# Every second w_in stage of a two-layer kernel by Strassen's scheme: seven half-width products and the additions between them

## The chip, the cores and the metric

The kernel runs on one core of a Trainium2 chip. The metric is the device time of one execution in microseconds. The core has a matrix engine (TensorE, in the profile PE, its weight loads PEld), VectorE (DVE), ScalarE (ACT), GpSimd (POOL) and SyncE (SP), whose queue issues the DMAs. SBUF is the working memory; PSUM, eight banks of 512 floats per partition, takes the matmuls' results.

## The reference, cut to what matters

```
qn = q / (norm(q, axis=1) + 1e-6); kn likewise        # q, k, v: 6016 x 256
a  = softmax(kn.T @ qn / tau)                         # 256 x 256
x  = v @ a                                            # 6016 tokens x 256
h  = x @ w_in;  g = h - tanh(h);  x = g @ w_out       # layer 0, w_in 256 x 2048
h  = x @ w_in2; g = where(h > 0, h, exp(min(h, 0)) - 1); out = g @ w_out2   # layer 1
```

Everything is float32.

## The kernel before

A short attention part makes `a`, and `a` is folded into layer 0's `w_in` (tiles `aw`). The rest is the two layers. The tokens are cut into 12 blocks of 512 columns (the last has 384), and the hidden dimension of 2048 into 8 parts p of 256. One step (layer, b, p) computes the part's h for a block, applies the activation, and adds its share of the output into the block's accumulator `o`; after p = 7 `emit_evac` copies `o` to SBUF (`osb`) and sends it off. Blocks 0 and 1 of layer 0 run interleaved while the weights arrive; from then on the steps run block by block.

Each operand of a matmul is split into a high part, rounded to the matrix engine's 32-bit format, and a low part, the remainder. A product is three matmuls: high by high, high by low, low by high. One step has 2 x 2 tiles of h, so 12 matmuls of 512 columns (`emit_h`, `product`), and 12 for `o` (`emit_out`). Every matmul loads its own 128 x 128 weights. The moving operand is read by `turned`, alternately from the two halves of the block, and the output is numbered accordingly; layer 0's eviction undoes this by a strided write.

The order is written out by hand: the loop over `order` emits h of step s, then `o` of step s - 2 (LAG = 2), then the activation (`emit_act`), and every engine runs its instructions in the order emitted. In layer 0 the activation is tanh on ACT, the subtraction on DVE, the cast to the high part (`ghi`, on DVE from block 3 on) and the low part (`glo`, DVE). In layer 1 it is relu, tanh and exp on ACT, two instructions on DVE (L635, L639), cast and low part on DVE. Both h and `o` have two PSUM buffers of two banks. All weights of both layers stay in SBUF; a `Converter` turns those of layer 1 into parts during layer 0, one unit per step (four DVE instructions, three on ACT, one on POOL).

Of the kernel before, what the change touches and what calls it, by code (L numbers as in the profile page):

```python
# [22 lines left out]
def kernel(  # L23
# [48 lines left out]
    class Converter:  # L72
        def __init__(self, stack, name, n, units, raws, nsq, nlow):
            self.nsq, self.nlow = nsq, nlow
# [39 lines left out]
        def second(self):  # L114

            if self.begun == self.at[1]:
                return []
            s = self.st[self.begun]
            self.begun += 1
            hz = self.tmp.tile([P, self.n], F32, tag="hz", name="hz")  # L120
            cut = self.tmp.tile([P, self.n], U32, tag="cut", name="cut")
# [76 lines left out]
    x_dram = [dram.tile([P, KC, n], F32, name=f"x{b}") for b, (_, n) in enumerate(blocks)]  # L198
    v_of = {}
# [52 lines left out]
    def evac_scalar(ps, m, fs):  # L252
        nc.scalar.activation(
            out=win_hi[0][:, m, fs], in_=ps[:, : 2 * P], func=AF.Copy, scale=rsum[:, m : m + 1]
        )

    def evac_vector(ps, m, fs):
        nc.vector.scalar_tensor_tensor(  # L258
            out=win_lo[0][:, m, fs], in0=ps[:, : 2 * P], scalar=rsum[:, m : m + 1],
            in1=win_hi[0][:, m, fs].bitcast(F32), op0=ALU.mult, op1=ALU.subtract,  # L260
        )
# [223 lines left out]
    with tc.manual_schedule():  # L485
        parts_of = attention()

        wpool2 = ctx.enter_context(tc.tile_pool(name="weights2", bufs=1, side="left"))
        win_hi[1] = wpool2.tile([P, KC, F], F32R, name="win_hi1")
        win_lo[1] = wpool2.tile([P, KC, F], F32R, name="win_lo1")  # L490
        gpool = ctx.enter_context(tc.tile_pool(name="g", bufs=2, side="left"))
        spool = ctx.enter_context(tc.tile_pool(name="s", bufs=2, side="left"))
        opool = ctx.enter_context(tc.tile_pool(name="o", bufs=2, side="left"))
        ps_h = ctx.enter_context(tc.tile_pool(name="ps_h", bufs=2, space=PSUM))
        out_stack = ctx.enter_context(ExitStack())
        ps_o = out_stack.enter_context(tc.tile_pool(name="ps_o", bufs=2, space=PSUM))
# [12 lines left out]
        def fold_attention(p):  # L509

            fs = slice(2 * P * p, 2 * P * (p + 1))
            if p == 1:
                ps = [ps_o.tile([P, 2, 512], F32, tag="o", name=f"aw{p}_{m}")[:, 0] for m in range(KC)]
            else:
                ps = ps_h.tile([P, 2, 512], F32, tag="h", name=f"aw{p}")
                ps = [ps[:, m] for m in range(KC)]
            for m in range(KC):
                if p == 1:
                    fold_half(ps[m], m, next_w, slice(0, 2 * P))
                else:  # L520
                    fold_half(ps[m], m, (win_hi[0], win_lo[0]), fs)
            return ps, fs
# [7 lines left out]
        def emit_h(layer, b, p, last=False):  # L530
            _, n = blocks[b]
            x_hi, x_lo = v_of[layer * NBLK + b]
            h = ps_h.tile([P, 2, 512], F32, tag="h", name=f"h{layer}_{b}_{p}")
# [4 lines left out]
            if layer == 0 and b + p < 2:  # L538

                w_hi, w_lo = [w[0][:, :, 2 * P * p : 2 * P * (p + 1)] for w in (win_hi, win_lo)]  # L540
# [14 lines left out]
            for i in range(2):  # L555
# [5 lines left out]
                            (win_hi[layer][:, c, fs], win_lo[layer][:, c, fs]),  # L561
# [6 lines left out]


        lower = []  # L570

        def emit_act(layer, b, p, h, fold, late=False, full=False):
# [41 lines left out]
            if layer == 0:  # L614
# [9 lines left out]
                if b > 2:  # L624
                    nc.vector.tensor_copy(out=hi, in_=g)  # L625
                else:
                    nc.scalar.activation(out=hi, in_=g, func=AF.Copy)  # L627
            else:

                e = late_pool[0].tile([P, 2, width], F32, tag="e", name="e")[:, :, :n]  # L630
                nc.scalar.activation(out=e, in_=h, func=AF.Relu, scale=-1.0)  # L631
                nc.scalar.activation(out=g, in_=e, func=AF.Tanh, scale=-0.5)  # L632
                nc.scalar.activation(out=e, in_=e, func=AF.Exp, scale=-1.0)  # L633
                between()
# [3 lines left out]
                fill(1)  # L638
                nc.vector.scalar_tensor_tensor(  # L639
                    out=g, in0=h, scalar=0.0, in1=g, op0=ALU.max, op1=ALU.add  # L640
                )
                fill(2)
                nc.vector.tensor_copy(out=hi, in_=g)  # L643
# [4 lines left out]
        def emit_last_act(b, p, h):  # L648
# [6 lines left out]
            for i in range(2):  # L655
                nc.scalar.activation(out=e[:, i], in_=h[i][:, :n], func=AF.Relu, scale=-1.0)
                nc.scalar.activation(out=g[:, i], in_=e[:, i], func=AF.Tanh, scale=-0.5)
                nc.scalar.activation(out=e[:, i], in_=e[:, i], func=AF.Exp, scale=-1.0)
# [4 lines left out]
                    out=g[:, i], in0=h[i][:, :n], scalar=0.0, in1=g[:, i], op0=ALU.max, op1=ALU.add  # L663
# [8 lines left out]
        def emit_last_out(b, p, g):  # L672
# [8 lines left out]
            for w, x, i, c in terms:  # L681
                nc.tensor.matmul(  # L682
                    out=columns(o[c][:, :n]), lhsT=w[1][:, 2 * p + i, c * P : (c + 1) * P],
# [10 lines left out]
        def emit_out(layer, b, p, g):  # L694
            _, n = blocks[b]
            if p == 0:
# [4 lines left out]
                else:  # L701
                    o = ps_o.tile([P, KC, 512], F32, tag="o", name=f"o{layer}_{b}")
# [7 lines left out]
            for w, x in terms:  # L710
                for i in range(2):
                    f = 2 * p + i
                    for c in range(KC):
                        nc.tensor.matmul(  # L714
                            out=columns(o[c][:, :n]),
                            lhsT=w[layer][:, f, c * P : (c + 1) * P],
# [5 lines left out]
        def emit_evac(layer, b, p):  # L722
# [5 lines left out]
            if layer == 0:  # L728

                nc.scalar.activation(  # L730
                    out=s.rearrange("p k (q u) -> p k u q", q=16),
                    in_=o.rearrange("p k (u q) -> p k u q", q=16),
                    func=AF.Copy,
                )
# [30 lines left out]
        for s, (layer, b, p) in list(enumerate(order))[3:]:  # L765
            if conv is not early and conv.done() and not late_pool:
                late_stack.close()
                pool = ctx.enter_context(tc.tile_pool(name="e", bufs=2, side="right"))
                late_pool.append(pool)
            if conv is early and early.done() and s >= starts[-1]:  # L770
                right.close()
                wlate = ctx.enter_context(tc.tile_pool(name="weights_late", bufs=1, side="right"))
                wout_hi[1] = wlate.tile([P, F // P, C], F32R, name="wout_hi1")
                wout_lo[1] = wlate.tile([P, F // P, C], F32R, name="wout_lo1")
                conv = Converter(late_stack, "l", NU // 2, late_units, 3, 1, 3)
# [4 lines left out]
            h = emit_h(layer, b, p, last=(s == len(order) - 1))  # L780
# [6 lines left out]
            if s < len(order) - 1:  # L787
                g = emit_act(layer, b, p, h, fold, full=(s < starts[-1]))
            else:
                g = emit_last_act(b, p, h)  # L790
            pend.append((layer, b, p, g))
            if done:
                emit_evac(*done[:3])

            if s == 3 or (s > 2 * NP and p == 1 and nv < len(phases)):
                load_v(nv)
            if s == 2 * NP - 2 or (s > 2 * NP and p == 4 and nv < len(phases)):
                split_v(nv)
                nv += 1
        emit_out(*pend[0])  # L800
        emit_last_out(*pend[1][1:])

# [34 lines left out]
```

## Time and profile before

| | |
|---|---|
| time, median of 3 runs | 1041.92 us (1041.63 to 1042.25) |
| the profiled execution's own time | 1041.79 us |
| its span in the trace | 1039.7 us |
| PE busy | 1032.8 us, 99% |
| PEld busy | 912.2 us, 88% |
| DVE busy | 842.7 us, 81% |
| ACT busy | 586.9 us, 56% |
| POOL busy | 69.8 us, 7% |

The span is what the trace covers; the time has some 2 us around it. Busy shares are means over all stages.

### The profile page before, as it was taken

How to read it: one execution, taken by the hardware profiler on the slowest of the kernel's cores; microseconds unless marked ns; L12 is line 12 of the kernel's file. 1: busy time of each engine (PE TensorE's matmuls, PEld its weight loads, DVE VectorE, ACT ScalarE, POOL GpSimd, SP SyncE). 2: the span in 40 equal slices, each digit the busy share in tenths (PEclk: the TensorE clock that was granted, in tenths of full speed). 3: DMA queues.
4: the chain of work that ended last, by engine and by line, in shares of the span. 5: the costliest groups of instructions: out<-in, count | busy, mean ns of one | idle time of the engine just before them, and what ended most of it. 6: DMA issues, size and time to landing. Idle time of an engine off the chain costs nothing.

```text
span 1039.7 us, 12840 instructions
## 1 busy us (share of the span) xinstructions
PE 1032.8 (99%) x4954; PEld 912.2 (88%) x4954; DVE 842.7 (81%) x926; ACT 586.9 (56%) x665; POOL 69.8 (7%) x65
## 2 busy tenths in 40 slices
PE   9999999999999999999999999999999999999998
PEld 8888888888888888888898888888888888888898
DVE  7899988888886666666667888888888888888887
ACT  7887776544433223222227666666666666666665
POOL 4522211111110000000000000000000000000000
PEclk9999999999999999999999999999999999999999
DMA  9723032212201101011011001011010010110100
GB/s 348 289 102 102 21 103 80 92 51 91 92 1 41 41 1 41 1 40 36 1 42 36 10 32 41 1 41 41 1 41 19 22 41 1 41 41 1 36 21 16
DMA packets 28381, 54.57 MB, mean 52 GB/s; under 512 B 2464, under 2 KB 7840, under 8 KB 28320
## 3 DMA queue, kind: packets, MB, share of 16 engines
q1 hardware_dynamic: 28032, 53.22, 15.0%
q8 instruction: 39, 0.64, 0.3%
q10 hardware_dynamic: 288, 0.52, 0.1%
q14 instruction: 22, 0.18, 0.1%
HBM read 41.42 MB, written 12.32 MB: 52 GB/s over the span
## 4 chain that ended last, share of the span: by engine, by line
PE 97%; DVE 2%; ACT 1%; issue 0%; DVEq 0%; ACTq 0%
PE h L243 46%; PE o L714 45%; PE S L311 4%; PE aw L243 1%; PE o_last L714 1%; DVE g L598 0%; DVE glo L593 0%; PE warm L323 0%; DVE cut L139 0%; DVE hz L127 0%; DVE cut L146 0%; PE o_last L682 0%; DVE win_lo L258 0%; DVE cut L133 0%; ACT g L597 0%
## 5 line engine op out<-in xcount | busy, mean ns | idle before, releaser
L243 PE MATMUL h<-vhi,win_hi 128*128 128x512 f32 (+1 forms) x754 | 282.5, 375 | 0.7 <-DVE g L598 0.7
L243 PE MATMUL h<-vlo,win_hi 128*128 128x512 f32 (+1 forms) x754 | 282.4, 375 | 0.0
L593 DVE TENSOR_TENSOR glo<-g,ghi 128x1024 fp32r<-128x1024 f32 (+1 forms) x191 | 236.8, 1240 | 22.8 <-ACT ghi L627 4.7
L243 PE MATMUL h<-vhi,win_lo 128*128 128x512 f32 (+1 forms) x754 | 221.0, 375 | 0.0
L615 ACT ACTIVATE g<-h 128x1024 f32<-128x1024 f32 (+1 forms) x82 | 82.3, 1003 | 233.2 <-PE h L243 233.2
L631 ACT ACTIVATE e<-h 128x1024 f32<-128x1024 f32 (+1 forms) x95 | 95.8, 1009 | 162.3 <-PE h L243 162.3
L714 PE MATMUL o<-ghi,wout_hi 128*128 128x512 f32 (+1 forms) x736 | 187.2, 377 | 0.0
L714 PE MATMUL o<-glo,wout_hi 128*128 128x512 f32 (+1 forms) x736 | 187.2, 377 | 0.0
L714 PE MATMUL o<-ghi,wout_lo 128*128 128x512 f32 (+1 forms) x736 | 187.1, 377 | 0.0
L616 DVE TENSOR_TENSOR g<-h,g 128x1024 f32<-128x1024 f32 (+1 forms) x82 | 98.2, 1198 | 93.6 <-ACT g L615 93.5
L243 PEld LDWEIGHTS h<-vhi,win_hi 128*128 128x128 f32 x754 | 142.5, 189 | 19.8 <-ACT wout_hi L166 1.1
L243 PEld LDWEIGHTS h<-vlo,win_hi 128*128 128x128 f32 x754 | 142.5, 189 | 18.6
L243 PEld LDWEIGHTS h<-vhi,win_lo 128*128 128x128 f32 x754 | 141.7, 189 | 18.5
L714 PEld LDWEIGHTS o<-ghi,wout_lo 128*128 128x128 f32 x736 | 138.5, 189 | 18.9
L714 PEld LDWEIGHTS o<-glo,wout_hi 128*128 128x128 f32 x736 | 138.5, 189 | 18.9
L714 PEld LDWEIGHTS o<-ghi,wout_hi 128*128 128x128 f32 x736 | 138.0, 189 | 18.5
L635 DVE SCALAR_TENSOR_TENSOR g<-e,g 128x1024 f32<-128x1024 f32 (+1 forms) x95 | 114.4, 1204 | 36.2 <-ACT e L633 35.6
L639 DVE SCALAR_TENSOR_TENSOR g<-h,g 128x1024 f32<-128x1024 f32 (+1 forms) x95 | 114.5, 1205 | 10.2 <-DVE g L635 0.5
L633 ACT ACTIVATE e<-e 128x1024 f32<-128x1024 f32 (+1 forms) x95 | 99.3, 1046 | 3.0
L632 ACT ACTIVATE g<-e 128x1024 f32<-128x1024 f32 (+1 forms) x95 | 99.3, 1045 | 3.0
L643 DVE CAST ghi<-g 128x1024 fp32r<-128x1024 f32 (+1 forms) x95 | 65.0, 685 | 10.1 <-DVE g L639 0.5
L625 DVE CAST ghi<-g 128x1024 fp32r<-128x1024 f32 (+1 forms) x72 | 48.8, 677 | 5.0
(139 smaller groups left out, 695.1 us busy)
## 6 DMA issues: line engine op xcount, KB each, us to landing
qk<-in_q_dram SPq DMA_DIRECT2D x23, 256.0 KB, 5.2
vraw<-in_vT_dram SPq DMA_DIRECT2D x11, 512.0 KB, 4.6
x<-osb SPq DMA_DIRECT2D x11, 512.0 KB, 3.0
vraw<-x SPq DMA_DIRECT2D x11, 512.0 KB, 4.0
out_dram<-osb SPq DMA_DIRECT2D x11, 512.0 KB, 2.9
qk<-in_k_dram SPq DMA_DIRECT2D x21, 256.0 KB, 5.3
raw0in<-in_moe_w_in_dram SPq DMA_DIRECT2D x8, 512.0 KB, 3.7
raw0out<-in_moe_w_out_dram SPq DMA_DIRECT2D x8, 512.0 KB, 3.7
```

The costliest lines, as they stand in the source:

```text
L243: nc.tensor.matmul(out=out, lhsT=w, rhs=x, start=(i == 0), stop=(i == len(pairs) - 1))
L593: nc.vector.tensor_tensor(out=lo, in0=g, in1=hi.bitcast(F32), op=ALU.subtract)
L615: nc.scalar.activation(out=g, in_=h, func=AF.Tanh)
L616: nc.vector.tensor_tensor(out=g, in0=h, in1=g, op=ALU.subtract)
L625: nc.vector.tensor_copy(out=hi, in_=g)
L631: nc.scalar.activation(out=e, in_=h, func=AF.Relu, scale=-1.0)
L632: nc.scalar.activation(out=g, in_=e, func=AF.Tanh, scale=-0.5)
L633: nc.scalar.activation(out=e, in_=e, func=AF.Exp, scale=-1.0)
L635: nc.vector.scalar_tensor_tensor(out=g, in0=e, scalar=1.0, in1=g, op0=ALU.add, op1=ALU.mult)
L639: nc.vector.scalar_tensor_tensor(out=g, in0=h, scalar=0.0, in1=g, op0=ALU.max, op1=ALU.add)
L643: nc.vector.tensor_copy(out=hi, in_=g)
L714: nc.tensor.matmul(out=columns(o[c][:, :n]), lhsT=w[layer][:, f, c * P : (c + 1) * P], rhs=turned(x[:, i]), start=(f == 0 and w is wout_hi ...
```

## The change

Blocks of 512 columns, from block 3 of layer 0 on and all of layer 1, compute the odd parts p (`PAIRS`) by Strassen's scheme in the Winograd form (`emit_h7`). The 2 x 2 tiles of weights and the 2 x 2 half blocks of tokens are combined to seven products instead of eight half-width ones: 7 x 3 = 21 matmuls of 256 columns into four one-bank tiles q0 to q3. One copy on ACT and four additions on DVE put h together in SBUF (`hs`). The sums of weights (`wsum`) and of tokens (`sum_v`, tiles t, thi, tlo) are made once per part or per block. Even parts stay as they were.

Around this: LAG is 3. From block 2 of layer 0 on, the class `Act` replaces `emit_act`: a plain step is activated in its own step, a Strassen step in the following plain step; the casts are on ACT, and the low part of a Strassen step on POOL. Layer 1's activation is exp and tanh straight from h, and the last DVE instruction takes min and max. PSUM holds q0 to q3 (four banks), one buffer of `o` (`ps_o`) and one of plain h (`ps_b`); plain blocks 0 to 2 and 11 have two h buffers instead of the q tiles. SBUF holds one layer's weights: the converted parts of layer 1 go to DRAM (`Converter.store`) and come back, part by part, during block 11 of layer 0. Conversion units are handled in plain steps only. `turned` now alternates within each half of a block, so layer 0's eviction is two instructions with a shorter stride.

```
+        def emit_h7(layer, b, p):
+            i = layer * NBLK + b
+            xq = [halves(x) for x in v_of[i]]
+            tq = t_of[i]
...
+            q1, q62, q57, q34 = [
+                ps_q[0].tile([P, 512], F32, tag=f"q{k}", name=f"q{k}_{layer}_{b}_{p}") for k in range(4)
+            ]
+            def product7(out, k, weights, moving, first, end):
+                out = out[:, k * W : (k + 1) * W].rearrange("p (l s) -> p l s", s=2)
+                hi, lo = [pair(y[:, moving[1]]) for y in moving[0]]
+                nc.tensor.matmul(out=out, lhsT=weights[0], rhs=hi, start=first, stop=False)
+                nc.tensor.matmul(out=out, lhsT=weights[0], rhs=lo, start=False, stop=False)
+                nc.tensor.matmul(out=out, lhsT=weights[1], rhs=hi, start=False, stop=end)
+            hs = steady[0].tile([P, 8, W], F32, tag="hs", name="hs", bufs=2)
...
+            product7(q1, 0, w(0, 0), (xq, 0), True, True)
+            nc.scalar.activation(out=hs[:, 3], in_=q1[:, :W], func=AF.Copy)
+            product7(q62, 0, ws(1), (tq, 1), True, False)
+            product7(q62, 1, w(1, 0), (xq, 2), False, True)
+            tt(out=hs[:, 0:8:4], in0=quads(q62), in1=two(3), op=ALU.add)
+            product7(q57, 0, ws(0), (tq, 0), True, False)
+            product7(q57, 1, ws(2), (tq, 2), False, True)
+            tt(out=hs[:, 1:3], in0=quads(q57), in1=two(0), op=ALU.add)
+            tt(out=hs[:, 7], in0=q57[:, :W], in1=hs[:, 2], op=ALU.add)
+            product7(q34, 0, ws(3), (xq, 3), True, False)
+            product7(q34, 1, w(1, 1), (tq, 3), False, True)
+            tt(out=hs[:, 5:7], in0=quads(q34), in1=hs[:, 1:3], op=ALU.add)
...
+        class Act:
...
+                    nc.scalar.activation(out=self.e, in_=h, func=AF.Exp)
+                    nc.scalar.activation(out=self.g, in_=h, func=AF.Tanh, scale=0.5)
...
+            def begin(self):
+                if self.layer:
+                    nc.vector.scalar_tensor_tensor(
+                        out=self.g, in0=self.e, scalar=1.0, in1=self.g, op0=ALU.add, op1=ALU.mult
+                    )
+                else:
+                    nc.vector.tensor_tensor(out=self.g, in0=self.h, in1=self.g, op=ALU.subtract)
+            def end(self):
+                if self.layer:
+                    nc.vector.scalar_tensor_tensor(
+                        out=self.g, in0=self.g, scalar=0.0, in1=self.h, op0=ALU.min, op1=ALU.max
+                    )
+            def upper(self):
+                nc.scalar.activation(out=self.hi, in_=self.g, func=AF.Copy)
+            def lower(self):
+                engine = nc.gpsimd if self.apart else nc.vector
+                engine.tensor_tensor(out=self.lo, in0=self.g, in1=self.hi.bitcast(F32), op=ALU.subtract)
...
+            h = emit_h7(layer, b, p) if seven else emit_h(layer, b, p, last=last)
...
+            if seven:
+                before.upper()
+                before.lower()
+                act = Act(layer, b, p, h)
...
+            else:
+                second = conv.second()
...
+                act = Act(layer, b, p, h[2][:, :, : blocks[b][1]])
+                if before and before.apart:
+                    before.begin()
+                    before.end()
+                    before.upper()
+                    before.lower()
...
+                if done:
+                    emit_evac(*done[:3])
+                for fill in second:
+                    fill()
...
+                act.begin()
+                act.end()
...
+                if p == 2:
+                    split_v_scalar(nv)
+                if p == 3:
+                    split_v_rest(nv, nc.vector)
+                apart = strassen(*phases[nv], PAIRS[0])
+                if p == 5 and apart:
+                    sum_v(nv, raw)
+                if p == 7:
+                    if apart:
+                        sum_v_rest(nv, nc.vector)
```

DVE's queue in block 5 of layer 1, before: parts 2 and 3 of that block (`h1_5_3` is h of part 3), with `e` and `g` the tiles of the activation.

```order
L593 TENSOR_TENSOR glo_6155<-g_6153,ghi_6154 128x1024
L635 SCALAR_TENSOR_TENSOR g_6189<-e_6192,g_6189 128x1024
L639 SCALAR_TENSOR_TENSOR g_6189<-h1_5_3_6164,g_6189 128x1024
L643 CAST ghi_6190<-g_6189 128x1024
L593 TENSOR_TENSOR glo_6191<-g_6189,ghi_6190 128x1024
```

The same place of the same queue in the changed kernel: the end of part 1 (Strassen, `hs_7280`), part 2 (plain, `h1_5_2`) and part 3 (Strassen, `hs_7373` from its q tiles).

```order
L712 SCALAR_TENSOR_TENSOR g_7321<-e_7322,g_7321 128x1024
L720 SCALAR_TENSOR_TENSOR g_7321<-g_7321,hs_7280 128x1024
L712 SCALAR_TENSOR_TENSOR g_7352<-e_7353,g_7352 128x1024
L720 SCALAR_TENSOR_TENSOR g_7352<-g_7352,h1_5_2_7327 128x1024
L684 TENSOR_TENSOR hs_7373<-q1_1_5_3_7370,hs_7373 128x2x256
L687 TENSOR_TENSOR hs_7373<-q2_1_5_3_7371,hs_7373 128x512
L688 TENSOR_TENSOR hs_7373<-q2_1_5_3_7371,hs_7373 128x256
L691 TENSOR_TENSOR hs_7373<-q3_1_5_3_7372,hs_7373 128x512
L729 TENSOR_TENSOR glo_7357<-g_7352,ghi_7356 128x1024
L250 TENSOR_TENSOR vlo18_7421<-vraw18_7274,vhi18_7367 128x1024
L712 SCALAR_TENSOR_TENSOR g_7415<-e_7416,g_7415 128x1024
```

The cast and one low part of every two are gone from DVE; four additions have come, and both activations of a pair stand ahead of them.

ACT's queue around the eviction of block 4 (`osb` from `o1_4`), before:

```order
L737 ACTIVATE osb_6122<-o1_4_5842 128x1024
L631 ACTIVATE e_6156<-h1_5_2_6127 128x1024
L632 ACTIVATE g_6153<-e_6156 128x1024
L633 ACTIVATE e_6156<-e_6156 128x1024
L631 ACTIVATE e_6192<-h1_5_3_6164 128x1024
```

And in the changed kernel, where `q0_1_5_3` is the first product of part 3 and `vhi18` the high part of the next block's input:

```order
L706 ACTIVATE g_7321<-hs_7280 128x1024
L705 ACTIVATE e_7353<-h1_5_2_7327 128x1024
L706 ACTIVATE g_7352<-h1_5_2_7327 128x1024
L725 ACTIVATE ghi_7325<-g_7321 128x1024
L893 ACTIVATE osb_7362<-o1_4_7030 128x1024
L243 ACTIVATE vhi18_7367<-vraw18_7274 128x1024
L681 ACTIVATE hs_7373<-q0_1_5_3_7369 128x256
L725 ACTIVATE ghi_7356<-g_7352 128x1024
L705 ACTIVATE e_7416<-hs_7373 128x1024
```

The eviction now stands one step later, behind a cast that needs part 1's activation, and ahead of the copy with which part 3's additions begin.

## Rows read from the trace of the kernel before

**Rows 1.** The page: the span, busy time by engine, a DMA of 512 KB.

```profile
span 1039.7 us, 12840 instructions
...
PE 1032.8 (99%) x4954; PEld 912.2 (88%) x4954; DVE 842.7 (81%) x926; ACT 586.9 (56%) x665; POOL 69.8 (7%) x65
...
vraw<-x SPq DMA_DIRECT2D x11, 512.0 KB, 4.0
...
```

**Rows 2.** Whom TensorE waited for: us in total, times, longest.

```profile
...
PE o_last L682 <- ACT ghi L666: 0.4, 1, 0.4
```

**Rows 3.** Busy us by engine in one stretch of layer 1, then the granted clock.

```profile
...
700.00:800.00 100.00, 100.00 (x465) 87.58 (x464) 86.95 (x80) 64.12 (x62) 0.00 (x0) 1.00 0.06 22
...
```

**Rows 4.** Timeline in layer 1: start us, us, engine, line, operation.

```profile
...
699.57 1.22 DVE L635 SCALAR_TENSOR_TENSOR g<-e,g 128x1024 f32<-128x1024 f32 x1
...
700.75 1.03 PE L714 MATMUL o<-ghi,wout_hi 128*128 128x512 f32 x4
700.89 1.23 DVE L639 SCALAR_TENSOR_TENSOR g<-h,g 128x1024 f32<-128x1024 f32 x1
700.96 1.02 ACT L631 ACTIVATE e<-h 128x1024 f32<-128x1024 f32 x1 [1.97 <-PE h L243]
...
705.93 1.03 PE L714 MATMUL o<-ghi,wout_hi 128*128 128x512 f32 x4
...
```

**Rows 5.** Instruction groups by shape: busy us, mean ns of one, idle before.

```profile
...
L243 PE MATMUL h<-vhi,win_hi 128*128 128x512 f32 x692 | 262.3, 379 | 0.7 <-DVE g L598 0.7
...
L730 ACT ACTIVATE osb<-o 128x1024 f32<-128x1024 f32 x11 | 22.4, 2038 | 11.0 <-PE o L714 11.0
...
L363 POOL TENSOR_TENSOR qk_lo<-qk,qk_hi 128x1024 fp32r<-128x1024 f32 x9 | 21.5, 2384 | 16.1 <-ACT qk_hi L362 14.8 <-DMA qk<-in_k_dram 0.6 <-DVE qk_hi L360 0.6
L243 PE MATMUL h<-vhi,win_hi 128*128 128x384 f32 x62 | 20.2, 326 | 0.0
...
L243 PE MATMUL aw<-next_w,aT_hi 128*128 128x256 f32 x8 | 1.3, 283 | 0.0
...
L466 ACT ACTIVATE aT_hi<-aT_ps 128x256 fp32r<-128x256 f32 x2 | 0.7, 374 | 0.2 <-PE aT_ps L462 0.2
...
L371 DVE TENSOR_TENSOR acc<-sq,acc 128x512 f32<-128x512 f32 x1 | 0.7, 692 | 0.1
...
```

**Rows 6.** Timeline of TensorE in a fold of the attention matrix.

```profile
...
53.94 0.64 PE L243 MATMUL aw<-next_w,aT_hi 128*128 128x256 f32 x4
...
54.66 0.64 PE L243 MATMUL aw<-next_w,aT_hi 128*128 128x256 f32 x4
...
```

**Rows 7.** Timeline of the weight loads near the attention's end.

```profile
...
40.56 0.98 PEld L393 LDWEIGHTS S<-ones,acc 128*128 128x128 f32 x8
...
43.00 0.52 PEld L418 LDWEIGHTS rq_ps<-diag,quot 128*128 128x128 f32 x4
...
```

**Rows 8.** Timeline of DVE and POOL in layer 0.

```profile
...
204.61 1.23 DVE L616 TENSOR_TENSOR g<-h,g 128x1024 f32<-128x1024 f32 x1 [0.62 <-ACT g L615]
...
204.96 0.74 POOL L173 TENSOR_TENSOR win_lo<-cut,win_hi 128x256 fp32r<-128x256 f32 x1 [4.44 <-ACT win_hi L166]
...
205.75 0.28 DVE L133 TENSOR_SCALAR cut<-hz 128x256 uint32<-128x256 uint32 x1
...
```

**Rows 9.** Timeline in layer 0, from DVE to ACT.

```profile
...
149.03 1.23 DVE L616 TENSOR_TENSOR g<-h,g 128x1024 f32<-128x1024 f32 x1 [0.80 <-ACT g L615]
...
150.35 1.06 ACT L627 ACTIVATE ghi<-g 128x1024 fp32r<-128x1024 f32 x1 [0.18 <-DVE g L616]
...
```

**Rows 10.** Timeline of ACT in layer 1, two instructions without a common tile.

```profile
...
609.86 1.06 ACT L633 ACTIVATE e<-e 128x1024 f32<-128x1024 f32 x1
610.83 1.04 ACT L216 ACTIVATE vhi<-vraw 128x1024 fp32r<-128x1024 f32 x1
...
```

**Rows 11.** Timeline of POOL and DVE while the weights are converted.

```profile
...
85.96 1.28 POOL L173 TENSOR_TENSOR win_lo<-cut,win_hi 128x512 fp32r<-128x512 f32 x1 [4.49 <-ACT win_hi L166]
...
86.27 2.06 DVE L593 TENSOR_TENSOR glo<-g,ghi 128x1024 fp32r<-128x1024 f32 x1
...
```

More of the change, by code (lines that the diff above doesn't have):

```diff
@@ L198 @@
     x_dram = [dram.tile([P, KC, n], F32, name=f"x{b}") for b, (_, n) in enumerate(blocks)]
+    in_dram = [dram.tile([P, 2, KC, 2, P], F32, name=f"in{p}") for p in range(NP)]
+    out_dram2 = [dram.tile([P, 2, 2, C], F32, name=f"out{p}") for p in range(NP)]
+    sums_dram = [dram.tile([P, 2, 4, P], F32, name=f"sums{j}") for j in range(len(PAIRS))]
     v_of = {}
@@ L532, in emit_h @@
             x_hi, x_lo = v_of[layer * NBLK + b]
-            h = ps_h.tile([P, 2, 512], F32, tag="h", name=f"h{layer}_{b}_{p}")
+            own = (layer, b) != phases[-1] and strassen(layer, b, 1)
+            h = (ps_b if own else ps_h).tile(
+                [P, 2, 512], F32, tag="o" if own else "h", name=f"h{layer}_{b}_{p}"
+            )
             if last:
@@ L567, in emit_h, with strassen, halves, sums_of @@
             return h
+        steady = []
+        def strassen(layer, b, p):
+            return blocks[b][1] == width and (layer > 0 or b > 2) and p in PAIRS
+        def halves(x):
+            return x.rearrange("p c (h t) -> p (c h) t", h=2)
+        def sums_of(p, first, second, away):
+            j = PAIRS.index(p)
+            t = steady[0].tile([P, 4, P], F32, tag="sum", name="sum")
+            sub = lambda o, a, b, op=ALU.subtract: nc.gpsimd.tensor_tensor(out=t[:, o], in0=a, in1=b, op=op)
+            sub(0, second[:, 0], second[:, 1], ALU.add)
+            sub(2, first[:, 0], second[:, 0])
+            sub(1, t[:, 0], first[:, 0])
+            sub(3, first[:, 1], t[:, 1])
+            dest = steady[0].tile([P, 2, 4, P], F32R, tag="sums_out", name="sums_out") if away else wsum[:, :, j]
+            nc.scalar.activation(out=dest[:, 0], in_=t, func=AF.Copy)
+            nc.gpsimd.tensor_tensor(out=dest[:, 1], in0=t, in1=dest[:, 0].bitcast(F32), op=ALU.subtract)
+            if away:
+                nc.sync.dma_start(out=sums_dram[j], in_=dest.bitcast(F32))
@@ L623, in emit_act @@
                 between()
[L624 to L627, printed above, removed]
+                nc.scalar.activation(out=hi, in_=g, func=AF.Copy)
             else:
                 e = late_pool[0].tile([P, 2, width], F32, tag="e", name="e")[:, :, :n]
[L631 to L634, printed above, removed]
+                nc.scalar.activation(out=e, in_=h, func=AF.Exp)
+                nc.scalar.activation(out=g, in_=h, func=AF.Tanh, scale=0.5)
                 nc.vector.scalar_tensor_tensor(
@@ L728, in emit_evac @@
             if layer == 0:
[L730 to L734, printed above, removed]
+                for c in range(KC):
+                    nc.scalar.activation(
+                        out=s[:, c].rearrange("p (h q u) -> p h u q", h=2, q=16),
+                        in_=o[:, c].rearrange("p (h u q) -> p h u q", h=2, q=16),
+                        func=AF.Copy,
+                    )
                 nc.sync.dma_start(out=x_dram[b], in_=s)
@@ L764 @@
         pend.append((*order[2], emit_act(*order[2], h2, None, full=True)))
[L765 to L769, printed above, removed]
+        for s, (layer, b, p) in list(enumerate(order))[3 : 2 * NP]:
             if conv is early and early.done() and s >= starts[-1]:
                 right.close()
[L772 to L775, printed above, removed]
+                steady.append(ctx.enter_context(tc.tile_pool(name="steady", bufs=1, side="right")))
+                wsum = steady[0].tile([P, 2, len(PAIRS), 4, P], F32R, name="wsum")
+                conv = Converter(late_stack, "l", NU // 2, late_units, 3, 1, 3, 3)
                 conv.load()
@@ L779 @@
                 conv.first()
-            h = emit_h(layer, b, p, last=(s == len(order) - 1))
+            h = emit_h(layer, b, p)
             fold = None
@@ L786 @@
                 emit_out(*done)
[L787 to L791, printed above, removed]
+            pend.append((layer, b, p, emit_act(layer, b, p, h, fold, full=(s < starts[-1]))))
             if done:
                 emit_evac(*done[:3])
-            if s == 3 or (s > 2 * NP and p == 1 and nv < len(phases)):
+            if s == 3:
@@ L800 @@
+        before.upper()
+        before.lower()
+        g = emit_last_act(b, p, h)
         emit_out(*pend[0])
-        emit_last_out(*pend[1][1:])
+        emit_out(*pend[1])
+        emit_last_out(b, p, g)
 def kernel(**inputs):
```

199 lines of the change are left out of this document (163 added, 36 removed).

## The prediction

> **What bounds the kernel now.** I read the page first, then what TensorE waits for, then the stages. TensorE (PE) is busy 1032.8 of the 1039.7 us span [rows 1]; it waits hardly at all, in the last activation for 0.4 us [rows 2]. So the time is the sum of the matmuls, and any other engine counts only if it makes PE wait. In layer 1 VectorE (DVE) is busy 87% and ScalarE (ACT) 64% at full granted clock [rows 3]: DVE is close behind. One plain step runs 5.18 us from one group of `o` matmuls to the next, 24 matmuls of 512 columns, 0.216 us each [rows 4]. The profiled execution took 1041.8 us, 2.1 more than its span, and lies 0.1 below the median of 1041.9; the sum is made against it.
>
> **What the change removes from PE.** 8 blocks of layer 0 (b = 3 to 10) and 11 of layer 1 have four Strassen stages each, 76 in all. A stage replaces 12 matmuls of 512 columns (12 x 0.216 = 2.59 us) by 21 of 256, each with its own weight load.
>
> What does such a matmul cost? Before has none with the interleaved moving operand, so two rows bound it. The fold `aw` (256 columns, same type, contiguous moving operand) goes at 0.72 / 6 = 0.120 us [rows 6]. The weight loads alone, beside matmuls of one column (`ones,acc`), go at (0.98 - 0.19) / 7 = 0.113 us, and beside matmuls of about the same length (`diag`) at (0.52 - 0.19) / 3 = 0.110 [rows 7], 0.19 being the length of one load row. Which is nearer? The record of an interleaved matmul is 379 ns at 512 columns and 326 at 384 [rows 5], 53 ns for 128 columns, so one of 256 should have 273. The `aw` records have 283 [rows 5]: a matmul that only waits to start need not be longer, so I read those 10 ns as the contiguous operand streaming more slowly, which the new products don't do. Then the loads set the pace, about 0.112 us. A stage is 21 x 0.112 = 2.35 us and saves 0.24; at 0.120 it is 2.52 and saves 0.07; the lower end is 0.109 by the columns (256 of 512 in half of 0.216, and a little), saving 0.30.
>
> The Trainium skill (TensorE: Matmul & The Clock Gate, section on LDWEIGHTS) gives a load of 128 columns as 128 / 1.2 = 107 ns; the trace's 110 to 113 is a little more. By that figure the columns would set the pace, and the layer-0 term below would be 9.6 instead of 7.7.
>
> **Does PE get its operands in time? Layer 1.** Here the order of DVE's queue decides. In a pair of steps it now holds: for the Strassen stage (S) the two halves of the activation (bS, eS), the same for the plain one (bP, eP), then four additions A, B, C, D that put the next S together, then the low part of P; the low part of S goes to GpSimd (POOL), and both casts go to ACT. An instruction that needs the one before it starts 1.32 us after it at 1024 elements (699.57 to 700.89) [rows 4], one that doesn't 1.14 (204.61 to 205.75) [rows 8]. 512 elements take 0.69 [rows 5], 256 by the same slope 0.42; so A to B 0.79, B to C 0.79, C to D 0.34, D 0.69, in all 2.61. Then ACT must do exponential and tanh of S before bS: 0.97 between independent ACT instructions and 1.06 for the second [rows 10], 0.09 from DVE's end to ACT's start [rows 9] and 0.03 back, 2.15. The ring is
>
> 2.61 (A to D) + 2.15 (ACT) + 1.32 (bS) + 1.14 (eS) + 1.32 (bP) + 1.14 (eP) = 9.68 us a pair.
>
> In it DVE rests only during the 2.15, less the low part of P. Per block come: the low part of the next input at p = 3 and of its sums at p = 7 (about 0.04 each beyond that rest); at p = 5 three additions for the sums, 1.65, of which 0.55 don't fit, and ACT's cast of them, which puts off the tanh of P by another 0.70; at p = 2 the cast of S, the eviction `osb` and the cast of the input stand on ACT ahead of the copy of q0 that A needs, 0.09 + 0.97 + 0.95 + 0.97 + 0.37 [rows 5, 9, 10] behind eS's end and 4.58 behind its start, where A would else begin at 3.60: 0.98. So a block's ring is 4 x 9.68 + 0.08 + 1.25 + 0.98 = 41.03 us. PE wants 4 x (5.18 + 2.59 + 2.35) = 40.5. Before, 8 x 5.18 = 41.44. **The ring binds in layer 1.** It holds PE at one place: the output accumulator has one buffer now, so the first `o` matmuls of a block (in step p = 3, after the 2.35 us of products) wait until ACT has evicted the block before, and that eviction stands behind the cast of S, behind eS. By my schedule it ends 0.9 us before PE wants it, so PE may run 0.9 ahead once. Elsewhere lateness is covered: the plain `h` bank is free 2.7 us early, `o` operands some 6 us, by the lag of three steps. Gain of layer 1: 11 x (41.44 - 41.03) + 0.9 = 5.4 us.
>
> **Layer 0.** One ACT and one DVE instruction less per activation: ring 2.61 + 1.13 + 1.14 + 1.14 = 6.0, with the four conversion instructions of a plain step (256 columns, some 0.42 each: 1.7) 7.7 a pair, under PE's 10.1. PE binds: 32 x 0.24 = 7.7. Against it: the strided eviction, 2.04 us before [rows 5], is now two instructions and starts some 0.2 after the last `o` matmul (as an `h` is picked up at 700.96, 0.21 after the `o` group began at 700.75 [rows 4]), so 0.2 + 2.04 + 0.1 = 2.34 meets the 2.35 of the products: taken as 0.1 a block, and 0.4 at the narrow block 11, 1.2 in all; bounds 0 and 8 x 0.7 if the shorter stride is slower. In block 2 the weight sums are made on POOL (per two steps two conversions of 0.74 [rows 8] and 1536 elements more, some 4 us at the 2.38 for 1024 [rows 5]) against DVE's instructions with two SBUF inputs: 1.0 taken, bounds 0 and 3. Net 5.5.
>
> **At nothing:** the reload of layer 1's weights by DMA (issued eight steps before use), stores of converted parts (SP issues them a step after they are ready), the copies of q0. Without that cover a reload of 0.5 MB would cost about what one of `vraw` takes, 4.0 us [rows 1], once. The **tail** gains 0.4: one more group of `o` lies over the last activation, where PE waited [rows 2].
>
> **Sum:** 5.4 + 5.5 + 0.4 = 11.3; 1041.8 - 11.3 = 1030.5 us; own range 1026 to 1035.
>
> **Rivals.**
> 1. *Products at the pace of `aw`, 0.120.* For it: same width, type and loads; against it the 10 ns. Then PE wants 4 x (5.18 + 2.59 + 2.52) = 41.2 a block, over the ring. Layer 1 gains 11 x 0.24 = 2.6, layer 0 2.2 less 1.5, tail 0.4: 3.7, **1038.1**.
> 2. *The ring does not bind* (ACT's chain shorter than I sum, or more slack before the eviction). 76 x 0.24 + 0.4 - 2.2 = 16.4: **1025.4**; with 0.109 a matmul 4.6 less, **1020.8**.
> 3. *Slower: POOL's low part of S catches a DVE instruction in every pair.* A DVE low part that began just after a POOL subtraction took 2.06 us, where 1024 elements else take 1.22 [rows 4, 11], while one with an input in PSUM (204.61) ran 1.23 beside POOL [rows 8]. POOL's 1024-element subtraction is 2.38 [rows 5]. In my order it begins behind bP and meets eP and A to D, each with one PSUM input; but if bP is late by the tanh it waits for, they collide. 0.84 a pair makes the ring 44.4 a block: 11 x 2.95 = 32.5 lost, less 5.9 kept, **1068.4**. The change loses as soon as a block's ring passes 41.44 + 5.9 / 11 = 41.98, that is 0.24 us a pair beyond my sum, whatever the cause.
>
> The Trainium skill (SBUF — State Buffer, section on who interferes with whom) states that rule: two SBUF inputs on DVE and a reading GpSimd instruction exclude one another, and the second waits. [rows 11] agrees.
>
> **How the numbers follow.** Forecast 0.40, rival 1 0.22, rival 2 0.16, rival 3 and other overruns of the ring 0.22. The before runs spread by 0.6 us, so 0.2% (2.1 us) is about what a measurement tells from no change. Forecast and rival 2 are faster but for 0.02; of rival 1, whose 1038.1 lies 1.7 inside that bound, 0.05 falls within 0.2% and 0.01 above; of rival 3 small overruns give 0.03 same and 0.19 slower. Faster 0.70, same 0.10, slower 0.20. The range runs from rival 2's lower end, 1021, to 1050, which takes in overruns up to about 0.45 a pair; above lie 0.13, below 0.06.
>
> **What would show it.** Starts of the 256-column products 0.112 apart (0.120: rival 1); S stages 4.94 us long in layer 0; in layer 1 PE idle once a block before the first `o`, ended by `osb`, with blocks of 41.0 us and DVE over 90% busy; no idle there would be rival 2, a low part or bS of about 2 us rival 3. PE idle elsewhere, at an `h` bank or a reloaded weight, would mean that I missed a wait.

## The result: slower, outside the range and of the other sign

The changed kernel takes 1056.49 us (median of 4 runs, 1055.08 to 1057.03) against 1042.07 before: ratio 1.0137, 95% interval [1.0119, 1.0154]. Forecast were 1030.5 and a range of 1021 to 1050. The profiled execution took 1056.99 us, 15.2 more than that of before. Its page, the lines that answer to [rows 1]; the third and fourth are TensorE's busy tenths and its granted clock in 40 slices:

```profile
span 1055.0 us, 14543 instructions
...
PE 1024.9 (97%) x5638; PEld 922.1 (87%) x5638; DVE 883.0 (84%) x1063; ACT 680.7 (65%) x850; POOL 284.7 (27%) x185
...
PE   9999997799999999999999999999999999999998
...
PEclk9999999899999999999999999999999999999999
```

PE's own work fell by only 7.9 us, and a span of which PE filled all but 6.9 us now has 30 us without it. The widest holes lie in two slices, 158 to 211 us: block 2 of layer 0. What PE waited for, answering to [rows 2] (total, times, longest):

```profile
PE h L270 <- DVE g L716: 14.0, 9, 2.4
PE q L672 <- DVE g L716: 6.0, 1, 6.0
PE o L869 <- ACT osb L886: 2.4, 1, 2.4
```

All three stand in layer 0 or at the change of layers. The stretches below run from the first output group of a block to that of the next: blocks 2, 3, 4 and 5 of layer 0, then blocks 0 and 3 of layer 1.

```profile
core 0: us, PE busy (x) PEld busy (x) DVE busy (x) ACT busy (x) POOL busy (x), PEclk, DMA share, GB/s
155.10:211.70 56.60, 44.29 (x211) 37.45 (x209) 47.46 (x57) 33.93 (x51) 26.30 (x32) 0.94 0.29 93
211.70:252.30 40.60, 40.59 (x229) 36.73 (x230) 35.17 (x51) 25.67 (x38) 13.44 (x9) 1.00 0.24 78
252.30:297.10 44.80, 42.38 (x230) 37.66 (x229) 33.73 (x49) 25.99 (x39) 15.55 (x13) 0.96 0.25 83
297.10:338.40 41.30, 41.09 (x231) 36.43 (x229) 37.60 (x48) 25.48 (x37) 12.15 (x8) 1.00 0.25 77
...
583.10:625.20 42.10, 42.06 (x228) 37.77 (x229) 36.87 (x41) 28.64 (x33) 10.00 (x5) 0.96 0.07 22
706.20:746.60 40.40, 40.40 (x230) 36.54 (x229) 36.75 (x41) 27.81 (x32) 9.58 (x5) 1.00 0.08 27
```

Layer 1, where [rows 3] had PE full as well, runs with PE full again, from its block 1 on at 40.46 us a block instead of 41.44. Block 2 of layer 0 takes 56.6, and up to block 8 the blocks there alternate between 40.6 to 41.3 and 43 to 45. Summed by stretches (starts of the output groups in both timelines):

| stretch | before, us | after, us | change | forecast |
|---|---|---|---|---|
| up to block 2's first output group | 151.6 | 155.1 | +3.5 | 0 |
| block 2 of layer 0 | 41.4 | 56.6 | +15.2 | +1.0 |
| blocks 3 to 11 of layer 0 | 362.7 | 371.4 | +8.7 | -6.5 |
| blocks 0 to 10 of layer 1 | 453.9 | 444.6 | -9.3 | -5.4 |
| the last block to the end of the span | 30.0 | 27.2 | -2.8 | -0.4 |

The first and last rows belong together: the lag of three steps puts an output group one input stage (2.59) later at the start and gives it back at the end; another 0.9 is there already at the first output group of all. The products themselves are as forecast, 0.11 us apart (ten such steps lie between these two starts):

```profile
346.60 0.28 PE L672 MATMUL q<-thi,wsum 128*128 128x256 f32 x1
...
347.71 0.28 PE L673 MATMUL q<-tlo,wsum 128*128 128x256 f32 x1
```

One of the waits, in block 6 of layer 0, on every engine:

```profile
346.47 0.43 DVE L130 SCALAR_TENSOR_TENSOR hz<-sq,raw1out 128x256 f32<-128x256 f32 x1
...
347.73 2.37 POOL L729 TENSOR_TENSOR glo<-g,ghi 128x1024 fp32r<-128x1024 f32 x1 [7.89 <-ACT ghi L725]
...
350.06 0.87 POOL L612 TENSOR_TENSOR sum<-cut 128x128 f32<-128x128 f32 x2
350.34 1.03 PE L869 MATMUL o<-glo,wout 128*128 128x512 f32 x4
...
350.96 0.53 DVE L136 TENSOR_SCALAR cut<-hz 128x256 uint32<-128x256 uint32 x1 [4.05 <-POOL sum L612]
...
351.91 0.63 ACT L618 ACTIVATE sums_out<-sum 128x512 fp32r<-128x512 f32 x1 [4.26 <-POOL sum L612]
...
352.54 1.22 DVE L716 TENSOR_TENSOR g<-h,g 128x1024 f32<-128x1024 f32 x1
...
353.81 0.48 PE L270 MATMUL h<-vhi,win 128*128 128x512 f32 x1 [2.44 <-DVE g L716]
```

Read it from the bottom. PE needs the bank that DVE's gelu subtraction (L716) frees. That stands behind the conversion of the next weights, which waits 4.05 us for a `cut` buffer that POOL's additions of the weight sums still read; ACT waits 4.26 us for the same additions. And POOL began them only after the low part of S (L729, 2.37 us). So one POOL queue, nearly idle before, holds both engines.

### The profile page after: what moved, and what is told of

It is laid out like the page before. It is cut to its first block, busy times and chain, and to the rows that moved or that the text cites. A ratio compares the mean times of both kernels' runs of the same rounds, so it can differ in the third digit from the quotient of the medians.

```text
span 1055.0 us, 14543 instructions
## 1 busy us (share of the span) xinstructions
PE 1024.9 (97%) x5638; PEld 922.1 (87%) x5638; DVE 883.0 (84%) x1063; ACT 680.7 (65%) x850; POOL 284.7 (27%) x185
## 4 chain that ended last, share of the span: by engine, by line
PE 71%; DVE 6%; ACT 3%; issue 1%; POOL 1%; DVEq 0%; ACTq 0%
PE o L869 35%; PE h L270 20%; PE q L673 5%; PE q L672 5%; PE q L674 5%; DVE g L716 2%; PE o_last L869 1%; DVE glo L729 1%; ACT osb L886 1%; ACT ghi L725 1%; POOL glo L729 1%; DVE vlo L250 1%; POOL sum L612 0%; DVE cut L142 0%; ACT vhi L243 0%
## 5 line engine op out<-in xcount | busy, mean ns | idle before, releaser
L869 PE MATMUL o<-ghi,wout 128*128 128x512 f32 (+1 forms) x1472 | 347.0, 379 | 2.5 <-ACT osb L886 2.4
L729 POOL TENSOR_TENSOR glo<-g,ghi 128x1024 fp32r<-128x1024 f32 x76 | 182.9, 2407 | 605.9 <-ACT ghi L725 482.1
L869 PEld LDWEIGHTS o<-ghi,wout 128*128 128x128 f32 x1472 | 272.0, 190 | 37.3 <-ACT osb L886 3.6
L270 PE MATMUL h<-vhi,win 128*128 128x512 f32 (+1 forms) x900 | 282.9, 376 | 14.8 <-DVE g L716 14.0
L725 ACT ACTIVATE ghi<-g 128x1024 fp32r<-128x1024 f32 (+1 forms) x175 | 182.4, 1042 | 87.1 <-DVE g L720 51.7
L270 PEld LDWEIGHTS h<-vhi,win 128*128 128x128 f32 x900 | 170.1, 190 | 41.0 <-DVE g L716 18.4
L869 PE MATMUL o<-glo,wout 128*128 128x512 f32 (+1 forms) x736 | 187.2, 377 | 0.0
L270 PE MATMUL h<-vlo,win 128*128 128x512 f32 (+1 forms) x450 | 168.5, 375 | 0.0
L869 PEld LDWEIGHTS o<-glo,wout 128*128 128x128 f32 x736 | 138.5, 189 | 18.9
L729 DVE TENSOR_TENSOR glo<-g,ghi 128x1024 fp32r<-128x1024 f32 (+1 forms) x99 | 119.0, 1202 | 36.6 <-ACT ghi L725 36.6
L712 DVE SCALAR_TENSOR_TENSOR g<-e,g 128x1024 f32<-128x1024 f32 (+1 forms) x95 | 114.2, 1202 | 23.5 <-ACT g L706 23.1
L705 ACT ACTIVATE e<-hs 128x1024 f32<-128x1024 f32 x44 | 46.6, 1059 | 67.5 <-DVE hs L691 67.5
L684 DVE TENSOR_TENSOR hs<-q,hs 128x512 f32<-128x512 f32 x76 | 52.2, 687 | 38.0 <-ACT hs L681 30.1
L716 DVE TENSOR_TENSOR g<-h,g 128x1024 f32<-128x1024 f32 (+1 forms) x48 | 56.3, 1174 | 18.7 <-ACT g L702 18.7
L720 DVE SCALAR_TENSOR_TENSOR g<-g,h 128x1024 f32<-128x1024 f32 (+1 forms) x51 | 60.4, 1185 | 5.7 <-DVE g L712 0.5
L672 PE MATMUL q<-thi,wsum 128*128 128x256 f32 x228 | 63.1, 277 | 0.0
L674 PE MATMUL q<-thi,wsum 128*128 128x256 f32 x228 | 63.0, 276 | 0.0
```

The source lines that it names most:

```text
L270: nc.tensor.matmul(out=out, lhsT=w, rhs=x, start=(i == 0), stop=(i == len(pairs) - 1))
L672: nc.tensor.matmul(out=out, lhsT=weights[0], rhs=hi, start=first, stop=False)
L674: nc.tensor.matmul(out=out, lhsT=weights[1], rhs=hi, start=False, stop=end)
L705: nc.scalar.activation(out=self.e, in_=h, func=AF.Exp)
L712: nc.vector.scalar_tensor_tensor(out=self.g, in0=self.e, scalar=1.0, in1=self.g, op0=ALU.add, op1=ALU.mult)
L716: nc.vector.tensor_tensor(out=self.g, in0=self.h, in1=self.g, op=ALU.subtract)
```

## Experiments

**The sums of weights left out, and each of their two waits by itself.** Edits: the calls of `own_sums` and `sums_of` and the reload removed, with `wsum` left at zero, so that PE does the same matmuls; or the cast of the sums moved from ACT to POOL; or a fourth `cut` buffer; or the last two together.

```diff
-            nc.scalar.activation(out=dest[:, 0], in_=t, func=AF.Copy)
+            nc.gpsimd.tensor_copy(out=dest[:, 0], in_=t)
...
-                conv = Converter(late_stack, "l", NU // 2, late_units, 3, 1, 3, 3)
+                conv = Converter(late_stack, "l", NU // 2, late_units, 3, 1, 3, 4)
```

> Leaves out all work on the sums of the weights: the additions of own_sums in block 2, those of sums_of in layer 0 for layer 1, their conversions, their stores and their reloads; wsum is set once to zero, so the products with a sum of weights multiply by zero. Theory (the making of the weight sums holds ACT and DVE behind POOL in layer 0): block 2 comes back from 56.6 to about 43 us between its first and the next block's first output group, and the three blocks of 44.8, 45.0 and 43.3 us come to about 41: 13 + 10 us, 1033 us in all. Rival (POOL's low part and the longer queues of layer 0 cost by themselves, or the handing over of the PSUM banks before the first products does): the stalls of 2.4 us stay, above 1048 us.

> ACT's conversion of the weight sums goes to POOL itself, so ACT no longer waits for POOL's additions; DVE still waits for the cut buffer that the additions read. Theory: block 2, where only ACT waits (3.1 us, four times), comes back by 9 to 12 us, and the three stalls of later blocks stay since DVE's wait of 4.05 us stands before the PE's: 1045 us. Rival (it is POOL's port against DVE in block 2, not the wait on ACT): block 2 stays at 52 us or more, within 4 us of 1056.5 in all.

> One more cut buffer, so that DVE's conversion of the next weights need not wait for POOL's additions; ACT's conversion of the sums still waits. Theory: block 2 stays at 56 us (its sums read no cut buffer), the three later blocks lose their 2.4 us stall and the low clock after it, 2 to 4 us each: 1047 us. Rival (ACT's wait holds the tanh or the q0 copy just as late): the stalls stay, 1056.

> Both edits: the sums converted on POOL, and one more cut buffer. All sums are still made. Theory: the two gains add, 10 to 12 in block 2 and 8 to 10 later, so 1034 to 1038 us, and faster than the kernel before; what stays is the wait when the PSUM banks are handed over ahead of block 3 (6.0 us now). Rival: POOL's longer chain (the conversion is its own now) delays its low part of S so that the output groups wait for it: above 1042.

Measured: no sums 1036.72 us (0.9951 [0.9936, 0.9965] of before), block 2 at 46.6 and blocks 3 to 8 at 41.0 to 41.4; the cast on POOL 1055.23; a fourth buffer 1053.69; both 1046.27. So the sums cost some 20 us, half of it in block 2. In the three later blocks with sums both waits hold: they take 43.6 to 43.9 us with the cast on POOL, 41.3 to 44.0 with the fourth buffer, 40.9 to 42.0 with both. But block 2 hardly moves (55.7 with the cast on POOL), so my first theory for it, ACT's wait for POOL, falls. There is a second cost there. DVE and POOL in block 2 with the cast on POOL:

```profile
161.22 1.32 POOL L627 TENSOR_TENSOR whole<-win 128x512 f32<-128x512 f32 x1
161.44 1.38 DVE L142 SCALAR_TENSOR_TENSOR cut<-hz,cut 128x256 uint32<-128x256 uint32 x1
...
163.35 1.21 DVE L716 TENSOR_TENSOR g<-h,g 128x1024 f32<-128x1024 f32 x1
...
166.31 2.13 POOL L619 TENSOR_TENSOR wsum<-sum,wsum 128x512 fp32r<-128x512 f32 x1
...
167.23 1.55 DVE L130 SCALAR_TENSOR_TENSOR hz<-sq,raw1in 128x256 f32<-128x256 f32 x1
...
170.37 1.22 DVE L716 TENSOR_TENSOR g<-h,g 128x1024 f32<-128x1024 f32 x1
```

and DVE without any sums:

```profile
161.75 1.22 DVE L716 TENSOR_TENSOR g<-h,g 128x1024 f32<-128x1024 f32 x1
...
165.29 0.48 DVE L130 SCALAR_TENSOR_TENSOR hz<-sq,raw1in 128x256 f32<-128x256 f32 x1
...
166.56 0.43 DVE L142 SCALAR_TENSOR_TENSOR cut<-hz,cut 128x256 uint32<-128x256 uint32 x1
...
167.37 1.22 DVE L716 TENSOR_TENSOR g<-h,g 128x1024 f32<-128x1024 f32 x1
```

From one gelu subtraction to the next DVE takes 5.62 us even without sums, more than PE's 5.18: subtraction, ACT's cast, low part and four conversions now stand in one chain. Beside POOL's additions the conversions with two SBUF inputs take 1.4 to 1.6 us instead of 0.4 to 0.5, and the chain 7.0 (6.6 to 7.0 in most steps of the block). That is [rows 11] in another place.

**Block 2 without conversions.** The conversion of layer 1's weights pauses there and goes on in block 3; then with the two repairs; then also with the eviction ahead of the cast of S in layer 1.

```diff
+                paused = (layer, b) == (0, 2)
-                second = conv.second()
+                second = [] if paused else conv.second()
...
+                    if layer and done:
+                        emit_evac(*done[:3])
                     before.upper()
...
-                if done:
+                if done and not (layer and before.apart):
                     emit_evac(*done[:3])
...
+                if not paused:
+                    conv.store()
...
```

> No conversion of layer 1's weights during block 2 (they go on in block 3); all sums are made, ACT converts them. Theory now: in block 2 a plain step is one chain through DVE and ACT, the subtraction of the gelu, ACT's cast, the low part, four conversions and the next subtraction, 5.6 us without POOL's additions beside it and 6.7 to 7 with them, against the 5.18 that TensorE takes. Without the conversions it is under 5.18: block 2 goes from 56.6 to 41 to 43 us, and the 6.3 us wait ahead of the first products goes with it; three stalls in later blocks stay or are even four: 1042 us. Rival (ACT's 3 us waits for POOL's additions make block 2 slow): block 2 stays above 50 us, 1052.

> The pause in block 2 together with the sums converted on POOL and one more cut buffer. Theory: block 2 at 41 to 42 us and the later blocks near 41 us, so 13 to 14 less than 1046.3: 1033 us. Rival (the wait at the handing over of the PSUM banks is the banks' own, not inherited lateness): 6 us of it stay, 1039.

> As pause_both, and in layer 1 ACT evicts the finished outputs ahead of the cast of S. Theory: the one wait of 2.4 us for osb, at the first output group of layer 1, shrinks by some 1.5 us with the low clock after it: 2 us less than pause_both, 1031. In the other blocks of layer 1 nothing changes (40.46 us each). Rival (ACT's cast comes 1 us later, and the chain of layer 1 has no slack): blocks of layer 1 grow by up to 1 us each, 10 us more.

Measured: 1044.77, 1036.15 and 1033.52 us (the last 0.9915 [0.9898, 0.9931] of before). Block 2 with the pause alone:

```profile
155.20:196.20 41.00, 41.00 (x210) 36.41 (x209) 30.68 (x32) 22.81 (x28) 16.27 (x17) 1.00 0.10 33
```

All four of its own sums are made, POOL now waits for ACT and not ACT for POOL, and PE has no hole; the 6.0 us ahead of the first products are gone too, so that wait was inherited. So block 2's 15.2 us need the conversions: 5.2 of them come without any sums, all of them with sums and conversions together, none with its sums alone. The pause also takes the conversions' work off ACT and POOL; that they cost time through DVE's chain is read from the rows above. How the 10 between divide into stretched instructions and ACT's wait stays open. Stalls move with the conversions. The change makes the first of layer 1's four sums in block 2; with the pause all four come later, in blocks 4, 6, 8 and 10. With the pause alone the first three of these take 43.8 to 44.7 us, and block 10 takes 40.95 where the change has 38.63; with the other two edits they take 40.7 to 42.4, and 38.75. The earlier eviction shortens the wait of 2.4 us at layer 1's first output group to 0.6, and layer 1 stays at 40.46 us a block.

**The moving operand in the order of memory.**

```diff
-                out = out[:, k * W : (k + 1) * W].rearrange("p (l s) -> p l s", s=2)
-                hi, lo = [pair(y[:, moving[1]]) for y in moving[0]]
+                out = out[:, k * W : (k + 1) * W]
+                hi, lo = [y[:, moving[1]] for y in moving[0]]
```

> The products' moving operands in the order of memory, not interleaved; their columns then stand in another order than those of the plain steps, so the output is another. Theory of the prediction (a contiguous fp32r operand streams more slowly than the interleaved one, as the 283 ns of aw against 273 suggested): products 0.120 us apart instead of 0.112, 21 x 0.008 = 0.17 us a stage, blocks of layer 1 at 41.1 us and 1068 us in all, less what the stalls of layer 0 hide. Rival (0.120 was the fold's own, its six matmuls too few): 0.112 as before, 1056.

Measured: 1066.37 us, blocks of layer 1 at 41.15. Its products stand 0.120 apart:

```profile
715.77 0.28 PE L674 MATMUL q<-thi,wsum 128*128 128x256 f32 x1
715.89 0.28 PE L672 MATMUL q<-thi,wsum 128*128 128x256 f32 x1
716.01 0.28 PE L673 MATMUL q<-tlo,wsum 128*128 128x256 f32 x1
```

That is the pace of the fold `aw` [rows 6], which also reads its operand in the order of memory. It bears out the prediction's reading of that row, though no run changed the order in the fold itself.

**The low part of S on DVE, right behind ACT's cast,** in layer 0, in layer 0 of pause_both_evac, and in layer 1.

```diff
-                engine = nc.gpsimd if self.apart else nc.vector
+                engine = nc.gpsimd if self.apart and self.layer else nc.vector
```

For layer 1 the condition is `self.apart and not self.layer`.

> The low part of S on DVE in layer 0 (layer 1 keeps it on POOL); all else as the change has it. Theory: two costs of layer 0 come from POOL's low part of 2.4 us: DVE's last conversion, with two SBUF inputs, takes 2.6 us beside it instead of 0.42, 2.2 us in every pair of steps that converts, and the sums' additions stand behind it in POOL's queue. On DVE the low part costs 1.14. Blocks of layer 0 at 41.3 us come to 40.5 and the three stalls of 2.4 us shrink to under 0.5: 3 x 3.5 + 5 x 0.8 = 14 less, 1042 us; block 2, which has no low part of S, stays at 56.6. Rival (DVE is the bound of layer 0, and an instruction more makes it later): blocks of layer 0 grow by 1 us or more, 1060.

> As pause_both_evac, with the low part of S on DVE in layer 0. Theory: the remaining 0.8 to 2 us a block of layer 0 go, blocks at 40.5 us throughout: 8 x 0.8 + some 3 = 6 to 9 less than 1033.5, 1026 us. Rival: blocks at 41.4 or more, 1034 or above.

> The low part of S on DVE in layer 1 (layer 0 keeps it on POOL). Theory (the ring of DVE and ACT in layer 1 stands just under TensorE's time: in a pair of 9.6 us DVE rests only where ACT makes exponential and tanh, and in three of four pairs another instruction fills that rest): 1.14 us more in those three pairs, blocks of 42.7 to 43.4 us instead of 40.46, 1080 to 1087 us. Rival (the ring has room, PE's 40.46 was never near it): blocks stay within 0.3 us of 40.46, 1057.

Measured: 1077.12, 1069.2 and 1143.34 us: all far slower than I expected, above all by one thing that I had left out. In layer 1:

```profile
761.34 1.23 DVE L720 SCALAR_TENSOR_TENSOR g<-g,hs 128x1024 f32<-128x1024 f32 x1
...
763.69 1.23 DVE L729 TENSOR_TENSOR glo<-g,ghi 128x1024 fp32r<-128x1024 f32 x1 [1.12 <-ACT ghi L725]
764.84 1.22 DVE L712 SCALAR_TENSOR_TENSOR g<-e,g 128x1024 f32<-128x1024 f32 x1
```

The instruction's place in DVE's queue is right behind the value that ACT must cast first. So DVE also waits 1.12 us: 3.50 from L720 to the next L712 instead of the 1.14 of [rows 8], 2.36 more in each pair. These runs say nothing of layer 0's stalls. Of layer 1 they say that its ring stood close: blocks of 48.42 us. Taken back by 4 x 2.36 the ring alone would be about 39.0 us (an estimate), under PE's 40.46.

**The same instruction on DVE in layer 0, at the end of the plain step,** where the cast is long made; alone, and on pause_both_evac. In pause_both_evac DVE's last conversion (L149) starts beside POOL's low part:

```profile
262.22 0.69 DVE L684 TENSOR_TENSOR hs<-q,hs 128x512 f32<-128x512 f32 x1 [0.42 <-ACT hs L681]
...
269.35 2.65 DVE L149 CUSTOM_DVE_ANT_0 cut<-cut,low 128x512 uint16<-128x512 uint16 x1
...
273.05 0.68 DVE L684 TENSOR_TENSOR hs<-q,hs 128x512 f32<-128x512 f32 x1
```

```profile
269.33 2.37 POOL L729 TENSOR_TENSOR glo<-g,ghi 128x1024 fp32r<-128x1024 f32 x1 [5.43 <-ACT ghi L725]
```

It takes 2.65 us and ends 0.3 after POOL does, and the pair, from one L684 to the next, 10.83 against PE's 10.12.

```diff
-            def lower(self):
-                engine = nc.gpsimd if self.apart else nc.vector
+            def lower(self, late=False):
+                own = self.apart and not self.layer
+                if own != late:
+                    return
+                engine = nc.gpsimd if self.apart and self.layer else nc.vector
...
                 act.begin()
                 act.end()
+                if before:
+                    before.lower(late=True)
```

> In layer 0 the low part of S on DVE again, but issued at the end of the plain step, behind the subtraction of its gelu, where ACT's cast has long been made (low_dve0 put it right behind the cast, and DVE waited 1.1 us for it in each pair). All else as the change has it. Theory (POOL's low part costs layer 0 by stretching a conversion by 2.2 us and by standing ahead of the sums): blocks of layer 0 that take 41.3 come to 40.5, those of 43 to 45 to 41 or so; block 2 stays at 56.6: 12 less, 1044 us. Rival (DVE's load in layer 0 is the bound): blocks at 42 us or more, 1060.

> The same move on pause_both_evac. Theory: the last conversion of a step takes 0.42 us again, blocks of layer 0 stand at 40.5 us, and 6 us go: 1027 us. Rival: blocks stay at 41.3 or above, 1033 or more.

Measured: 1044.2 us alone, 12.3 less than the change as it is; 1025.29 us on the repaired version (1025.05 to 1025.6; 0.9841 [0.9824, 0.9857] of before, faster than both kernels). L149, first in the change, then in best_late0 (count, busy us, mean ns):

```profile
L149 DVE CUSTOM_DVE_ANT_0 cut<-cut,low 128x512 uint16<-128x512 uint16 x32 | 29.8, 930 | 1.1
```

```profile
L149 DVE CUSTOM_DVE_ANT_0 cut<-cut,low 128x512 uint16<-128x512 uint16 x32 | 13.9, 433 | 1.1
```

Blocks 3 and 4 of layer 0 in best_late0, then block 4 in late0, without the other repairs:

```profile
196.10:236.60 40.50, 40.50 (x231) 36.64 (x230) 35.66 (x52) 25.74 (x38) 2.99 (x4) 1.00 0.25 78
236.60:277.10 40.50, 40.50 (x230) 36.64 (x230) 37.71 (x54) 25.78 (x37) 7.07 (x10) 1.00 0.28 92
```

```profile
254.10:294.50 40.40, 40.40 (x229) 36.55 (x228) 37.56 (x53) 26.12 (x38) 7.37 (x10) 1.00 0.28 91
```

DVE runs four instructions more in each of these blocks than in pause_both_evac (52 and 54 instead of 48 and 50), is busy less (35.66 and 37.71 us instead of 37.59 and 40.23), and PE has no hole: it was POOL's instruction, beside and ahead of others, not DVE's load. In late0 the three blocks with sums are at 40.5 as well, and neither DVE nor ACT waits for the additions there: without the low part ahead of them they make nobody late.

## Why the prediction failed, by its own steps

The step that failed is the sum for layer 0, with its "PE binds": it was to gain 5.5 us net, and layer 0 from block 2 on lost 23.9 (15.2 and 8.7 in the table). Two terms make nearly all of this, block 2 and the sums of layer 1's weights. The prediction had named the sign of such a miss, "PE idle elsewhere, at an `h` bank".

- **The products: right.** 0.112 us, what the weight loads alone take [rows 7], and not the 0.120 of [rows 6]. The record forecast at 273 ns has 275 to 277. A block of four pairs was summed to 40.5 and measured 40.46 wherever PE isn't held.
- **"The ring binds in layer 1": wrong, on the safe side.** 41.03 us were summed; the ring is below 40.46, and rival 2 holds for layer 1, which gains 9.3 us instead of 5.4. Terms that were too large: the pair, 9.58 against 9.68 where DVE runs without a rest, and p = 5, 10.60 against 10.93. These are small, but a bound 1.4% above PE's time chose the wrong case.
- **"With the four conversion instructions ... 7.7 a pair, under PE's 10.1. PE binds": wrong, though cheap by itself.** It took durations of conversions alone. One of them meets POOL's low part and takes 2.2 us more, and a pair that also holds the low part of the next input's sums takes 10.83. Blocks 3, 5 and 7, which make no sums of weights, lie 0.1 to 0.8 us over 40.46, 1.8 together. This is rival 3's mechanism, priced for layer 1 alone, where every instruction that meets POOL reads PSUM. In layer 0 the conversions don't.
- **The sums of layer 1's weights weren't in the sum at all.** They are queued on POOL behind its low part, with ACT and DVE waiting: three blocks of 43.3 to 45.0 us, some 11.7 over 40.46 (with the stretched conversions that they hold too).
- **"In block 2 the weight sums are made on POOL ... 1.0 taken, bounds 0 and 3": 15.2.** The term priced stretched instructions, but not the chain that they lie in, which at 5.6 us a step was over PE's 5.18 even before anything stretched.
- **The narrow block 11, 0.4:** 2.4 us of wait and a granted clock of 0.96 over the next 42 us; with the eviction ahead of the cast of S the wait was 0.6.
- The range's upper end, 1050, came from overruns of layer 1; for layer 0 the bounds were summed to some 9 us.

The Trainium skill (SBUF — State Buffer, section on who interferes with whom) says that of a DVE instruction with two SBUF inputs and a GpSimd instruction that reads SBUF the second waits until the first is done; L149's 2.65 us beside POOL's 2.37 agrees. The prediction cited that rule and applied it to layer 1's pairs and, as 1.0 us, to block 2, but not to the conversions beside POOL's low part in layer 0.

## What to carry to other kernels

When work moves to an idle engine, list every instruction that stands behind it in that queue and everything that waits for those, also in stages whose own time has room. Where a rule names a pair of instructions that exclude each other, go through all queues for such pairs, not only that of the stage thought to bind. Putting an instruction on another engine is half of an edit; the other half is the place where its input is ready, which made 1077 us into 1044.

## What was not expected of the hardware

A wait of PE for 2.44 us was followed by one clock in one block and by another in the next but one. Around the waits in blocks 6 and 8 of layer 0:

```profile
349.00:353.80 4.80, 2.36 (x11) 1.72 (x10) 2.72 (x4) 1.88 (x6) 3.98 (x6) 1.00 0.00 0
353.80:358.00 4.20, 4.19 (x12) 3.36 (x13) 4.05 (x6) 2.11 (x2) 0.79 (x2) 0.59 0.75 250
436.00:440.10 4.10, 1.66 (x9) 1.12 (x7) 2.82 (x5) 1.27 (x4) 3.28 (x6) 1.00 0.00 0
440.10:444.30 4.20, 4.20 (x20) 3.69 (x21) 4.03 (x7) 2.05 (x2) 0.74 (x2) 1.00 0.49 187
```

After the first the granted clock was 0.59 on the mean over 4.2 us, near the lower of its two levels (1.2 and 2.4 GHz), and 12 matmuls ran in place of 20; after the second it stayed at 1.00. The blocks took 44.96 and 43.27 us: by these two, a hole of 2.4 us cost 2.4 or some 4. What decided between them no run shows.

A contiguous fp32r operand of 256 columns streams more slowly than the interleaved one: some 285 ns a record and 0.120 us apart, against 275 to 277 and 0.112.
